# Second layer in quarters, most of its float64 weights converted beside it; twelve whole additions a pair feed summing products over three operands

## The chip, the core and the metric

The kernel runs on one core of a Trainium2 chip. TensorE (PE) multiplies matrices from on-chip memory (SBUF) into accumulators (PSUM); VectorE (DVE), ScalarE (ACT) and GpSimd (POOL) work on tiles element by element, POOL on SBUF alone; SyncE's queue (SP) issues the transfers (DMA). Each engine takes its instructions strictly in the order in which they were issued, so an instruction that waits holds up all that stand behind it on its engine. The metric is the device time of one execution in microseconds (us), as the median of the runs.

## The reference, cut to what matters

```python
q_pool = q.reshape(B, H, S // 2, 2, D).mean(axis=3)           # B 4, H 8, S 1152, D 64
attn = softmax(q_pool @ k.T / sqrt(D))                        # per head 576 x 1152
x = (attn @ v)                                                # 2304 tokens x 512
logits = x @ phi                                              # 32 slots, 4 for each of 8 experts
slot_input = softmax(logits, over tokens).T @ x
slot_out[e] = relu(slot_input[e] @ w1[e]) @ w2[e]             # w1, w2: 32 MB together
x = softmax(logits, over slots) @ slot_out                    # 2304 x 512
h = x @ w_in                                                  # w_in 512 x 2048, float64
g = where(h >= 1, h, where(h <= -1, 0, (h + 1) ** 2 / 4))
out = g @ w_out                                               # w_out 2048 x 512, float64
```

## The kernel before, in words

The program has three stages, and its instructions are issued by hand in the order in which they are to run.

**Attention.** Two heads make a pair `P`; there are 16 pairs, each of 9 steps `c` (128 keys) with two slots `h`. `at(g, slot, ...)` puts an action into a slot of step `g = 9 P + c`; "(c, h)" is a slot of a pair in what follows. A slot issues, in this order: the score products `mx` of a pair 11 steps ahead (`max_half`, line 305) and DVE's row maximum over them (line 317); this pair's scores `st` (line 371) and ACT's exponential `e` of them (line 376); at some slots the summing products (`es_sum`, line 394); the products with the values, `acc` (line 401); and then whatever was put into the slot. `mx`, `st` and some transposes share three PSUM buffers (`sc_p`), so the `st` of a slot takes the buffer that the `mx` of the slot ahead of it had, and must wait until DVE has read that `mx`.

The denominators are sums of `e` over the keys. `es_add` (line 384) adds the `e` tiles of several steps on DVE into `es`; `es_sum` multiplies the resulting operands with a column of ones on PE. `ADD` says in which slot which step's `e` is added, whole (0 to 2) or by halves; `GRP` groups the steps: 0 to 4 are added into one operand, 5, 6, 7 and 8 are operands of their own. `TAT` puts three operands behind the `st` of slot (7, 0) and two behind that of slot (0, 0) of the next pair. `PREP` places the preparation of later pairs (`prep_klo`, `prep_qp`, `prep_qlo`: four DVE instructions a pair).

**Conversion.** `w_in` and `w_out` come as float64. Each of 32 chunks of 128 x 512 is loaded (`cv_load`), and turned into float32 by one ACT instruction (`cv_abs`, line 191) and four on DVE (`cv_step`, lines 198 to 206: two with one operand and a constant, two with two operands). `CVS` puts all 32 into slots of the attention. The result goes back to DRAM (`wo_dr`, `wi_dr`) and is read again at the start of the last stage.

**Experts.** `w_load` fetches the 32 tiles of `w1` and `w2`, 1 MB each, into slots that `NWA` to `NW4` count, 23 of them; `w_last` goes into a tile that comes free later. The remaining 8 tiles, and behind them `wi_dr`, each wait until an earlier tile has been used (`w_used`). `h1` and `s2o` (lines 775, 827) are the products with `w1` and `w2`.

**Out stage.** `M = slot_out @ w_in` (line 924) is computed for all 2048 columns, so that `h = c @ M`; it is split in a high and a low part and repeated over partition groups (`Mrep`). Each of 9 blocks of 256 tokens has four units of 512 columns: products `h` (lines 968, 1014), an activation from ACT and DVE instructions (`h_unit`, `g_unit`), a split of the result into `ghi` (ACT) and `glo` (POOL, line 987, from two tiles in SBUF), and 24 products `po` (lines 1031 to 1033) with the split `w_out` (`whi`, `wlo`), which accumulate in PSUM over the four units of a block. `w_split` (lines 905, 907) makes `whi` and `wlo` on ACT, POOL and DVE at the start of the stage. `unit_step` runs the activations some units ahead of the products.

## Time and profile before

| | us |
|---|---|
| median of 3 runs (lowest, highest) | 782.45 (780.24, 783.18) |
| profiled execution, span from first to last instruction | 785.9 |
| attention, to the last summing products | 0 to about 502 |
| experts, to the last `s2o` | about 502 to 546 |
| start of the out stage | 546 to 573.6 |
| out stage, products without a break | 573.6 to 783 |

The profiled execution has no device time of its own beside its span, which lies 3.45 us above the median of the runs. PE is busy in 96% of the span, DVE in 74%, ACT in 57%, POOL in 16%. Busy times count an instruction from its start to its end; neighbours on one engine overlap by a little, so that the distance from one start to the next is less than the duration. In the view of stretches each engine has its busy time and, in brackets, its instructions, then follow the clock granted to TensorE (1.00 is 2.4 GHz, 0.50 is 1.2 GHz), the busy share of the DMA engines, and GB/s. In the view in order of time a row has start, duration, engine, line, operation, result and operands, shape and count, and in brackets the idle time ahead of it and what ended it; several instructions in a row can stand as one.

### The profile page before, as it was taken

To read this page: it belongs to the slowest core of one execution; us is meant where nothing else is said; L and a number is where in the kernel's file an instruction comes from. 1 tells how busy PE (TensorE), PEld (TensorE's weight loads), DVE (VectorE), ACT (ScalarE), POOL (GpSimd) and SP (SyncE) were. 2 spreads that over 40 slices of the span, in tenths; PEclk is the share of its full clock that TensorE was granted. 3 is DMA by queue.
4 is the path that set the end of the run, shared out by engine and by line. 5 is a ranking of instruction groups with operands and counts; after the bars stand their busy time and mean duration, and the time that the engine had idled before them with its cause. 6 is when DMAs were issued, how large, how long until landed. Compare 5 with 4: busy or idle time off the path is not lost.

```text
span 785.9 us, 19049 instructions
## 1 busy us (share of the span) xinstructions
PE 757.1 (96%) x7896; PEld 556.6 (71%) x7896; DVE 581.4 (74%) x947; ACT 451.7 (57%) x855; POOL 125.9 (16%) x100
## 2 busy tenths in 40 slices
...
GB/s 215 201 174 137 182 193 205 206 248 200 186 233 203 183 260 164 188 263 180 212 263 134 222 96 237 269 333 395 241 0 28 28 28 20 7 28 28 27 28 28
DMA packets 138263, 127.11 MB, mean 162 GB/s; under 512 B 80576, under 2 KB 100288, under 8 KB 137408
## 3 DMA queue, kind: packets, MB, share of 16 engines
...
HBM read 87.10 MB, written 13.11 MB: 128 GB/s over the span
## 4 chain that ended last, share of the span: by engine, by line
PE 60%; DMA 2%; DVE 2%; ACT 2%; issue 1%; SPq 0%; ACTq 0%; DVEq 0%
PE acc L401 9%; PE st L371 9%; PE po L1031 8%; PE po L1032 8%; PE po L1033 8%; PE mx L305 4%; PE acc L394 3%; DMA wi<-wi_dr 2%; PE h L968 2%; PE h L775 2%; PE tx L439 1%; PE tb L466 1%; DVE r L1021 1%; PE tr L428 1%; PE lp L482 0%
## 5 line engine op out<-in xcount | busy, mean ns | idle before, releaser
L376 ACT ACTIVATE e<-st 128x576 f32<-128x576 f32 x288 | 187.0, 651 | 139.0 <-PE st L371 125.6
L317 DVE TENSOR_REDUCE mp<-mx 128x1 f32<-128x576 f32 x282 | 212.1, 754 | 44.9 <-PE mx L305 38.0
L401 PE MATMUL acc<-e,vf 128*64 128x288 f32 x1152 | 195.1, 411 | 0.5 <-ACT e L376 0.5
L305 PE MATMUL mx<-K,q 128*64 128x288 f16 x1152 | 124.8, 298 | 9.6 <-DVE mp L317 3.4
L371 PE MATMUL st<-q,K 128*64 128x288 f16 x1152 | 122.0, 288 | 5.9 <-ACT e L376 4.7
L371 PE MATMUL st<-q,S 128*64 128x288 f16 x1152 | 122.0, 287 | 0.0
L305 PEld LDWEIGHTS <-q 128*64 128x64 f16 x1152 | 66.3, 112 | 70.2 <-issue 24.5
L1031 PE MATMUL po<-whi,ghi 128*128 128x512 f32 (+1 forms) x280 | 108.5, 388 | 0.0
L1032 PE MATMUL po<-wlo,ghi 128*128 128x512 f32 (+1 forms) x280 | 108.5, 388 | 0.0
L1033 PE MATMUL po<-whi,glo 128*128 128x512 f32 (+1 forms) x280 | 108.0, 386 | 0.0
L981 DVE TENSOR_TENSOR r<-cl,r 128x1024 f32<-128x1024 f32 x34 | 80.6, 2372 | 36.9 <-ACT cl L980 36.9
L987 POOL TENSOR_TENSOR glo<-r,ghi 128x1024 fp32r<-128x1024 f32 x34 | 82.2, 2417 | 95.3 <-ACT ghi L986 95.3
L401 PEld LDWEIGHTS acc<-e,vf 128*64 128x64 f32 x1152 | 77.4, 137 | 8.3 <-ACT e L376 2.0
L371 PEld LDWEIGHTS <-K 128*64 128x64 f16 x1152 | 68.3, 110 | 20.9 <-issue 12.7
L752 POOL MEMSET xfer<- 128x1024 f32 x1 | 1.0, 957 | 493.5 <-PE pb L562 493.5
L384 DVE TENSOR_TENSOR es<-es,e 128x288 f32<-128x288 f32 (+1 forms) x144 | 77.5, 550 | 2.2 <-ACT e L376 2.2
L371 PEld LDWEIGHTS <-S 128*64 128x64 f16 x1152 | 69.3, 110 | 3.4
L971 ACT ACTIVATE r<-h,cols 128x512 f32<-128x512 f32 x68 | 43.0, 685 | 31.4 <-PE h L968 31.4
L1033 PEld LDWEIGHTS po<-whi,glo 128*128 128x128 f32 x280 | 53.2, 190 | 10.8
L1031 PEld LDWEIGHTS po<-whi,ghi 128*128 128x128 f32 x280 | 53.4, 191 | 9.8
L1032 PEld LDWEIGHTS po<-wlo,ghi 128*128 128x128 f32 x280 | 53.3, 190 | 9.3
L972 DVE TENSOR_SCALAR cl<-h 128x512 f32<-128x512 f32 x68 | 43.8, 685 | 15.8 <-ACT r L971 13.9
(191 smaller groups left out, 854.1 us busy)
## 6 DMA issues: line engine op xcount, KB each, us to landing
...
```

The lines of the kernel that those rows point to most:

```text
L305: nc.tensor.matmul(ps[p0:p1, i, 0:HQ], lhsT=q1[P][:, t, p0:p1], rhs=kk[:, j * HQ:(j + 1) * HQ], start=True, stop=True)
L317: nc.vector.tensor_reduce(out=mp[P][:, t, a:a + 1], in_=ps[:, :, 0:HQ], op=ALU.max, axis=AX.XY)
L371: nc.tensor.matmul(ps[c0:c0 + 64, i, 0:HQ], lhsT=kk[:, ci, c0:c0 + 64], rhs=f[:, sl[i]], start=first, stop=not first)
L376: nc.scalar.activation(out=e, in_=ps[:, :, 0:HQ], func=AF.Exp, scale=ESC)
L384: nc.vector.tensor_tensor(out=Es[P, n, h][:, i0:i1], in0=a[:, i0:i1], in1=b[:, i0:i1], op=ALU.add)
L401: nc.tensor.matmul(acc[P, i][h * 64:(h + 1) * 64, 0:HQ], lhsT=vt[P][:, h, c, :], rhs=E[P, c, h][:, i, :], start=(c == 0), stop=(c == NK - ...
L972: nc.vector.tensor_scalar(out=cl[:, a:b], in0=src, scalar1=-1.0, scalar2=1.0, op0=ALU.max, op1=ALU.min)
L981: nc.vector.tensor_tensor(out=r[:, sl], in0=cl[:, sl], in1=r[:, sl], op=ALU.add)
L987: nc.gpsimd.tensor_tensor(out=glo[n, qd][:, sl], in0=r[:, sl], in1=ghi[n, qd][:, sl].bitcast(F32), op=ALU.subtract)
L1031: nc.tensor.matmul(po, lhsT=ghi[n, qd][:, j, sl], rhs=whi[:, f, cs], start=(f == 0), stop=False)
L1032: nc.tensor.matmul(po, lhsT=ghi[n, qd][:, j, sl], rhs=wlo[:, f, cs], start=False, stop=False)
L1033: nc.tensor.matmul(po, lhsT=glo[n, qd][:, j, sl], rhs=whi[:, f, cs], start=False, stop=(f == 15))
```

## The change

**Attention.** Steps 0 to 6 are added into one operand: twelve whole additions a pair, one in each slot from (2, 0) to (7, 1), where eight whole ones' worth were done in twelve instructions. The summing products have three operands, all behind the `st` of slot (0, 0) of the next pair. Of the conversions 12 of 32 chunks stay in the attention: two instructions a pair in the first slots, and one in each slot from step 6 of pair 14. The preparation moves by a few slots. **Experts.** Three tiles fewer are loaded ahead (20 instead of 23), and 11 instead of 8 wait for an earlier tile; `wi_dr` and `wo_dr` are gone, the converted weights stay in SBUF (`Wst`). **Out stage.** It runs over quarters `q` of the 2048 columns, and in a quarter over the 9 blocks: 36 units `k`. `M` is made a quarter at a time (`m_mm`, `m_rep`), each unit's 24 products end in PSUM and are added on DVE to partial results in SBUF (`o_out`). The other 20 chunks are converted in the units that `CVB` names, and split by `w_hi` (ACT) and `w_lo` (DVE). The activation is h clipped below at -1 plus (1 - clip(h)) squared over 4: two DVE instructions with an operand from PSUM take the place of one of 1024 columns from SBUF, and in odd units ACT clips.

```diff
-NWA, NW0, NW1, NW2, NWK, NW3, NW4 = 10, 2, 1, 6, 1, 2, 1
+NWA, NW0, NW1, NW2, NWK, NW3, NW4 = 10, 2, 1, 3, 1, 2, 1
...
+AHEAD = 3
+CVB = 1, 2, 3, 4, 5, 6, 7, 8, 9, 10, 11, 13, 14, 15, 17, 18, 19, 21, 22, 24
+MB = {1: 2, 2: 10, 3: 20}
...
-CVS = (0, 0), (0, 1), (1, 0), (1, 1), (3, 1), (7, 0), (7, 1), (8, 0), (8, 1)
+CVS = (0, 0), (0, 1)
+CVL = 4, 6
...
-GRP = ((0, 1, 2, 3, 4), (5,), (6,), (7,), (8,))
-TAT = ((7, 0, (1, 2, 0)), (9, 0, (3, 4)))
-ADD = ((4, 1, 0, 0, 2), (5, 1, 1, 0, 1), (6, 1, 1, 1, 2), (6, 2, 0, 0, 2), (7, 2, 1, 0, 2), (8, 3, 0, 0, 1), (9, 3, 0, 1, 2),
-       (10, 3, 1, 0, 2), (10, 4, 0, 0, 1), (11, 4, 0, 1, 2), (12, 4, 1, 0, 1), (13, 4, 1, 1, 2))
-PREP = (-20, -18, (-34, -33), -36, -16, -30), (-24, -22, (-41, -37), -41, -19, -37)
+GRP = ((0, 1, 2, 3, 4, 5, 6), (7,), (8,))
+TAT = (9, 0, (0, 1, 2)),
+ADD = tuple((2 * c + h + 2, c, h, 0, 2) for c in range(1, 7) for h in range(2))
+PREP = (-20, -18, (-34, -33), -36, -16, -30), (-24, -22, (-38, -36), -37, -18, -34)
...
-    wlist += [("wi", dc, 0) for dc in range(4)]
-    wo_dr = dr_p.tile([128, 16, DM], F32, name="wo_dr")
-    wi_dr = dr_p.tile([4, 128, DFF], F32, name="wi_dr")
...
+        qd, x = divmod(n, 8)
+        if x < 4:
+            src = w_in[x * 128:(x + 1) * 128, qd * 1024:(qd + 1) * 1024]
+            r0 = (4 * qd + x - 4) * 128
+            src = w_out[r0:r0 + 128, :]
+        nc.sync.dma_start(out=f64b[n % 2], in_=src.rearrange("p (f t) -> p f t", t=2))
+        cv[n] = f64b[n % 2], Wst[:, x - 4 if x >= 4 else 4 + 4 * (qd % 2) + x, :]
...
-            if n < 16:
-                nc.sync.dma_start(out=wo_dr[:, n, :], in_=dst)
-            else:
-                dc, qr = divmod(n - 16, 4)
-                nc.sync.dma_start(out=wi_dr[dc][:, qr * 512:(qr + 1) * 512], in_=dst)
-            if n + 3 < 32:
-                cv_load(n + 3)
+            if n + 2 < 32:
+                cv_load(n + 2)
...
-        cvs = [(NK * P + c, sl) for P in range(NP - 1) for c, sl in
-               CVS][CV0:]
-        for n in range(32):
+        for j in range(4):
+            at(NK * NP - 8 + j, 1, sel_build, j)
+        g1_ = NK * (NP - 1) - 3
+        cvs = [(NK * P + c, sl) for P in range(1, NP) for c, sl in CVS if NK * P + c < g1_]
+        cvs += [(g, sl) for g in range(g1_, NK * NP - 1) for sl in range(2)]
+        for n in range(12):
...
-        pieces = [(0, 2), (2, 4), (4, 8), (8, 12), (12, 16)]
-        for f0, f1 in pieces:
-            nc.sync.dma_start(out=wlo[:, f0:f1, :].bitcast(F32), in_=wo_dr[:, f0:f1, :])
...
+            if e < 4:
+                w_hi(0, e)
+            if 0 < e <= 4:
+                w_lo(0, e - 1)
...
+        def m_mm(q):
+            ps = po_tile(f"M{q}")[:, 0:128]
+            for dc in range(4):
+                for j in range(4):
+                    nc.tensor.matmul(ps[32 * j:32 * j + 32], lhsT=soT[:, dc, :],
+                                     rhs=Wst[:, 4 + 4 * (q % 2) + dc, j * 128:(j + 1) * 128], start=(dc == 0), stop=(dc == 3))
+            nc.scalar.activation(out=Mhl[:, 0], in_=ps, func=AF.Copy)
+            nc.vector.tensor_tensor(out=Mhl[:, 1], in0=ps, in1=Mhl[:, 0].bitcast(F32), op=ALU.subtract)
+        def m_rep(q):
+            Mst[q] = m_p.tile([128, 4, 128], F32R, tag="Mst", name=f"Mst{q}")
+            for a in range(2):
+                ps = po_tile(f"Mr{q}_{a}").rearrange("p (j x n) -> p j x n", j=2, x=2)
+                for j in range(2):
+                    nc.tensor.matmul(ps[:, j], lhsT=Sel[:, 2 * a + j, :], rhs=Mhl, start=True, stop=True)
+                for x, p0 in ((0, 0), (1, 64)):
+                    dst, src = Mst[q][p0:p0 + 64, 2 * a:2 * a + 2], ps[p0:p0 + 64, :, x]
+                    if x:
+                        nc.vector.tensor_copy(dst, src)
+                    else:
+                        nc.scalar.activation(out=dst, in_=src, func=AF.Copy)
...
+        def h_unit(k):
+            cl = t_p.tile([128, 4, TB], F32, tag="cl", name=f"cl{k}")
+            ps = []
+            for a in (0, 2):
+                ps.append(h_mm(k, a, a + 2))
+                if k % 2:
+                    nc.scalar.activation(out=cl[:, a:a + 2], in_=ps[-1], func=AF.Relu, scale=-1.0, bias=ones)
+                else:
+                    nc.vector.tensor_scalar(out=cl[:, a:a + 2], in0=ps[-1], scalar1=-1.0, scalar2=1.0, op0=ALU.max, op1=ALU.min)
...
+        def g_unit(k):
+            cl, ps = hq[k]
+            if k % 2:
+                nc.scalar.activation(out=cl, in_=cl, func=AF.Relu, scale=-1.0, bias=two)
+                nc.scalar.activation(out=cl, in_=cl, func=AF.Square, scale=-0.5, bias=ones)
+            else:
+                nc.scalar.activation(out=cl, in_=cl, func=AF.Square, scale=-0.5, bias=half)
+            r = hq[k] = t_p.tile([128, 4, TB], F32, tag="r", name=f"r{k}")
+            for a in (0, 2):
+                nc.vector.scalar_tensor_tensor(out=r[:, a:a + 2], in0=ps[a // 2], scalar=-1.0, in1=cl[:, a:a + 2], op0=ALU.max, op1=ALU.add)
...
+        def o_out(k, tt, po, c0=0, w=DM):
+            q, n = SEQ[k]
+            t = PA[2 * n + tt][:, c0:c0 + w]
+            if q:
+                nc.vector.tensor_tensor(out=t, in0=po, in1=t, op=ALU.add)
+            elif tt:
+                nc.vector.tensor_copy(t, po)
+            else:
+                nc.scalar.activation(out=t, in_=po, func=AF.Copy)
+            if q == 3:
+                r0 = n * TB + tt * 128
+                nc.sync.dma_start(out=out[r0:r0 + 128, c0:c0 + w], in_=t)
...
+            sp = split_of(k - 1)
+            ahead(k + AHEAD + 1)
+            if sp:
+                w_hi(*sp)
+            conv(k, 0, 2)
+            if k < len(SEQ) - 1:
+                o_part(k, 0, pos[0])
+                for q, b in MB.items():
+                    if k == b:
+                        m_mm(q)
+                    if k == b + 1:
+                        m_rep(q)
+                o_out(k, 0, pos[0])
+                conv(k, 2, 4)
+                if sp:
+                    w_lo(*sp)
+                o_part(k, 1, pos[1])
+                o_out(k, 1, pos[1])
+                conv_abs(k + 1)
```

On DVE, slots (6, 1) to (8, 1) of pair 7, before; `mx` and `mp` are the row maxima, `es` the additions, `mm` and `qn` close the maxima of a pair, `kn` and `qf` are preparation, `wst` conversion.

```order
L317 TENSOR_REDUCE mp_3656<-mx_8_1_4118 128x1
L350 TENSOR_TENSOR mm_4124<-mp_3656 128x9
L352 TENSOR_SCALAR qn_0_103<-mm_4124 128x9
L384 TENSOR_TENSOR es_0_1_3932<-es_0_1_3932,e_4_1_4041 128x288
L260 SCALAR_TENSOR_TENSOR kn_4075<-kf_3963,kn_4075 128x9x64
L273 TENSOR_TENSOR qf_3966<-qf_3966 128x9x64
L317 TENSOR_REDUCE mp_4145<-mx_0_0_4146 128x1
L206 SCALAR_TENSOR_TENSOR wst_3834<-f_15_3366,wst_3834 128x512
L317 TENSOR_REDUCE mp_4145<-mx_0_1_4195 128x1
L198 TENSOR_SCALAR wst_4193<-wst_4193 128x512
L317 TENSOR_REDUCE mp_4145<-mx_1_0_4215 128x1
```

And in the changed kernel, the same slots.

```order
L304 TENSOR_REDUCE mp_3450<-mx_8_1_3882 128x1
L337 TENSOR_TENSOR mm_3888<-mp_3450 128x9
L339 TENSOR_SCALAR qn_0_103<-mm_3888 128x9
L371 TENSOR_TENSOR es_0_1_3699<-es_0_1_3699,e_5_1_3856 128x576
L304 TENSOR_REDUCE mp_3907<-mx_0_0_3908 128x1
L371 TENSOR_TENSOR es_0_0_3673<-es_0_0_3673,e_6_0_3877 128x576
L304 TENSOR_REDUCE mp_3907<-mx_0_1_3928 128x1
L371 TENSOR_TENSOR es_0_1_3699<-es_0_1_3699,e_6_1_3902 128x576
L304 TENSOR_REDUCE mp_3907<-mx_1_0_3948 128x1
L247 SCALAR_TENSOR_TENSOR kn_3839<-kf_3729,kn_3839 128x9x64
L304 TENSOR_REDUCE mp_3907<-mx_1_1_3968 128x1
L260 TENSOR_TENSOR qf_3732<-qf_3732 128x9x64
```

Ahead of the maximum of slot (7, 0), the first with `mx_0_0`, stand `mm`, `qn` and a whole addition, where `mm`, `qn`, half an addition and two preparations stood. Each of the next two slots has a whole addition (the tail of the longer `es`) where a conversion instruction stood, and the preparations now stand one to a slot in step 8.

On SP's queue, the last loads of the experts and those of the out stage, before.

```order
L133 DMA w_3_1_8244<-in_moe_w_dram 128x4x512
L133 DMA w_4_1_8262<-in_moe_w_dram 128x4x512
L133 DMA w_5_1_8270<-in_moe_w_dram 128x4x512
L133 DMA w_6_1_8279<-in_moe_w_dram 128x4x512
L133 DMA w_7_1_8286<-in_moe_w_dram 128x4x512
L133 DMA wi_0_8292<-wi_dr 128x2048
L133 DMA wi_0_8298<-wi_dr 128x2048
L133 DMA wi_0_8313<-wi_dr 128x2048
L138 DMA wi_0_8325<-wi_dr 128x4x256 x2
L900 DMA wlo<-wo_dr 128x1024 x2
L900 DMA wlo<-wo_dr 128x2048 x3
```

And in the changed kernel, from `w_last` to the last tile of `w2`.

```order
L131 DMA w_last<-in_moe_w_dram 128x4x512
L131 DMA w_5_0_7767<-in_moe_w_dram 128x4x512
L131 DMA w_6_0_7773<-in_moe_w_dram 128x4x512
L131 DMA w_7_0_7779<-in_moe_w_dram 128x4x512
L131 DMA w_0_1_7785<-in_moe_w_dram 128x4x512
L131 DMA w_1_1_7803<-in_moe_w_dram 128x4x512
L131 DMA w_2_1_7811<-in_moe_w_dram 128x4x512
L131 DMA w_3_1_7820<-in_moe_w_dram 128x4x512
L131 DMA w_4_1_7827<-in_moe_w_dram 128x4x512
L131 DMA w_5_1_7833<-in_moe_w_dram 128x4x512
L131 DMA w_6_1_7839<-in_moe_w_dram 128x4x512
L131 DMA w_7_1_7854<-in_moe_w_dram 128x4x512
```

Eleven tiles of `w2` stand behind `w_last`, where eight tiles and four megabytes of `wi` stood (before, `w_5_0` to `w_7_0` stand ahead of `w_last`). Nothing of `wi` and `wlo` is left.

On DVE in the out stage, two units before (`cl` and `r` belong to the activation).

```order
L972 TENSOR_SCALAR cl_0_9236<-h_0_0_9237 128x512
L972 TENSOR_SCALAR cl_0_9236<-h_0_1_9242 128x512
L981 TENSOR_TENSOR r_3_9193<-cl_3_9194,r_3_9193 128x1024
L972 TENSOR_SCALAR cl_1_9286<-h_1_0_9287 128x512
L972 TENSOR_SCALAR cl_1_9286<-h_1_1_9292 128x512
L981 TENSOR_TENSOR r_0_9235<-cl_0_9236,r_0_9235 128x1024
```

And in the changed kernel, unit 10, which converts a chunk and splits another (`Wst` conversion, `wlo` split, `pa` the additions to the partial results).

```order
L967 SCALAR_TENSOR_TENSOR r_8981<-h_0_8916,cl_8915 128x512
L967 SCALAR_TENSOR_TENSOR r_8981<-h_2_8920,cl_8915 128x512
L190 TENSOR_SCALAR Wst<-Wst 128x512
L192 TENSOR_SCALAR Wst<-Wst 128x512
L1029 TENSOR_TENSOR pa_8053<-po_0_8965,pa_8053 128x512
L195 SCALAR_TENSOR_TENSOR Wst<-f_0_74,Wst 128x512
L198 SCALAR_TENSOR_TENSOR Wst<-f_0_74,Wst 128x512
L890 TENSOR_TENSOR wlo_7947<-Wst,whi_7946 128x512
L1029 TENSOR_TENSOR pa_8054<-po_1_8966,pa_8054 128x512
```

A unit had two instructions from PSUM and one addition of two SBUF tiles. Now it has two that read PSUM and SBUF, five that read SBUF alone, and two additions that wait for the unit's products.

## Rows read from the trace of the kernel before

**Rows 1.** Stretches: attention pair, experts, start of out stage, rest (core 0).

```profile
331.40:359.10 27.70, 27.70 (x386) 20.28 (x383) 26.24 (x48) 19.09 (x41) 0.00 (x0) 1.00 1.03 230
516.00:546.00 30.00, 29.85 (x275) 9.05 (x276) 12.55 (x47) 2.04 (x3) 5.24 (x33) 1.00 1.03 383
560.00:580.00 20.00, 15.95 (x61) 12.20 (x60) 17.04 (x25) 16.49 (x30) 15.74 (x12) 0.83 0.08 35
573.60:783.00 209.40, 209.00 (x1014) 176.63 (x1012) 127.92 (x103) 121.69 (x158) 88.92 (x38) 0.99 0.06 23
```

**Rows 2.** In order of time, PE, slots (0, 0) to (1, 0) and (7, 0) of a pair.

```profile
330.98 0.41 PE L305 MATMUL mx<-K,q 128*64 128x288 f16 x4
331.81 1.19 PE L394 MATMUL acc<-e,cols 128*32 128x192 f32 x32
333.46 0.41 PE L305 MATMUL mx<-K,q 128*64 128x288 f16 x4
334.68 0.41 PE L305 MATMUL mx<-K,q 128*64 128x288 f16 x4
...
352.10 0.41 PE L305 MATMUL mx<-K,q 128*64 128x288 f16 x4
355.07 0.41 PE L305 MATMUL mx<-K,q 128*64 128x288 f16 x4
```

**Rows 3.** In order of time, DVE, the same pair.

```profile
333.92 0.76 DVE L317 TENSOR_REDUCE mp<-mx 128x1 f32<-128x576 f32 x1 [0.18 <-PE mx L305]
334.59 0.68 DVE L203 SCALAR_TENSOR_TENSOR wst<-f,wst 128x512 int32<-128x512 int32 x1
...
352.12 0.17 DVE L350 TENSOR_TENSOR mm<-mp 128x9 f32<-128x9 f32 x1
352.33 0.19 DVE L352 TENSOR_SCALAR qn<-mm 128x9 f16<-128x9 f32 x1
352.41 0.45 DVE L384 TENSOR_TENSOR es<-es,e 128x288 f32<-128x288 f32 x1
352.78 0.75 DVE L260 SCALAR_TENSOR_TENSOR kn<-kf,kn 128x576 f16<-128x576 f32 x1
353.44 0.75 DVE L273 TENSOR_TENSOR qf<-qf 128x576 f32<-128x576 f32 x1
```

**Rows 4.** Groups by line and shape, 100 to 450 us; busy us, mean ns.

```profile
L384 DVE TENSOR_TENSOR es<-es,e 128x576 f32<-128x576 f32 x36 | 27.0, 750 | 0.0
L200 DVE TENSOR_SCALAR wst<-wst 128x512 int32<-128x512 int32 x27 | 11.3, 418 | 0.0
```

**Rows 5.** In order of time, SP's queue, last loads of the experts.

```profile
517.13 12.90 SPq L133 DMA_DIRECT2D w<-in_moe_w_dram  x8
534.71 3.50 SPq L138 DMA_DIRECT2D wi<-wi_dr  x2
```

**Rows 6.** In order of time, from the last `s2o` into the out stage.

```profile
545.87 0.69 DVE L910 COPY Prun<-s2o 128x512 f32<-128x512 f32 x1 [1.54 <-PE s2o L827]
548.32 1.07 PE L924 MATMUL M<-wi,soT 128*32 128x256 f32 x16
553.60 0.64 PE L924 MATMUL M<-wi,soT 128*32 128x256 f32 x8 [0.84 <-DMA wi<-wi_dr]
555.64 0.50 PE L1014 MATMUL h<-cT,Mst 128*128 128x256 f32 x2
559.92 0.62 PE L1040 MATMUL po<-whi,ghi 128*128 128x512 f32 x2
573.65 0.63 PE L1031 MATMUL po<-whi,ghi 128*128 128x512 f32 x1
```

**Rows 7.** Instructions of one line in the out stage: count, ns min/median/max.

```profile
L981 DVE TENSOR_TENSOR r<-cl,r x34: 1209/2421/2493, 576.4 to 751.7; 128x1024 f32<-128x1024 f32 x34
L987 POOL TENSOR_TENSOR glo<-r,ghi x34: 2391/2404/2849, 578.8 to 755.4; 128x1024 fp32r<-128x1024 f32 x34
L972 DVE TENSOR_SCALAR cl<-h x68: 676/682/692, 571.7 to 745.1; 128x512 f32<-128x512 f32 x68
```

**Rows 8.** In order of time, DVE and POOL in one unit of the out stage.

```profile
644.75 2.41 POOL L987 TENSOR_TENSOR glo<-r,ghi 128x1024 fp32r<-128x1024 f32 x1 [3.19 <-ACT ghi L986]
645.82 2.43 DVE L981 TENSOR_TENSOR r<-cl,r 128x1024 f32<-128x1024 f32 x1 [1.35 <-ACT cl L980]
```

309 lines of the change are left out of this document (120 added, 189 removed).

## The prediction

> **What bounds the kernel now.** I read the view of stretches first, to know which stage has which limit, then the order of time inside a pair of the attention, around the last loads of the experts and at the start of the out stage, and last the durations of single lines. In a pair of the attention (27.7 us) PE is busy throughout and DVE for 26.2; in the experts PE and the DMA engines are both full, at 383 GB/s; at the start of the out stage PE stands for a fifth of the time and the granted clock falls to 0.83; after that PE is full for 209 us, with DVE busy for 128, ACT for 122 and POOL for 89 [rows 1]. So PE is the bound in attention and out stage, and what I need to know is whether DVE, which the change loads differently, stays behind it. In the attention a slot without extras lasts 1.22 us (333.46 to 334.68); slot (0, 0) with two operands of summing products lasts 2.48, and slot (7, 0) with three 2.97 [rows 2]: 1.26 and 1.75 us for the products. All five are PE's time, nothing waits in them.
>
> **The attention, part by part.** The change leaves one place with three operands: 1.75 instead of 3.01 us a pair, **1.26 us less on PE in each of 16 pairs, 20.2 us** if nothing else moves.
>
> On DVE a maximum has .76 us, and the next instruction starts .67 after it; two preparations start .66 apart for .75 each [rows 3]. So an instruction costs its duration less some .08: whole addition .67 (750 ns), half one .37 (452 ns), conversion .60 or .34 [rows 3, 4]. Per pair: additions before 4 x .67 + 8 x .37 = 5.6, now 12 x .67 = 8.0; conversions before some 9 slots, 2.25 x (2 x .60 + 2 x .34) = 4.2, now a quarter of that, .9. DVE gets .9 us less work in a pair, PE 1.26 less: as a sum, DVE still fits.
>
> By slots it does not. In each of the slots (2, 0) to (7, 1) DVE now has a maximum and a whole addition, 1.34 us, where PE needs 1.22 unless transposes lengthen the slot, and in step 8 a preparation keeps it at 1.33. With three PSUM buffers the `st` of a slot needs the maximum of the slot ahead to be finished. A maximum starts .46 after its `mx` at the earliest (333.46 and 333.92 [rows 2, 3]), ends .76 later, and the `st` of the next slot is due 1.22 + .24 after that `mx`, so DVE may be late by about .2. Slot (5, 1) follows transposes and starts on time. Then the lag is .12 in (6, 0) and .24 in (6, 1); `mm` and `qn` (.3 together [rows 3]) and an addition make it about .7 in (7, 0). Before, this was the place of the three summing operands, which gave DVE 1.75 us behind a worse pile (`mm`, `qn`, half an addition, two preparations, to 354.11); they have moved away. PE waits .5 us there, and .12 more in each of (7, 1), (8, 0), (8, 1); slot (0, 0), now with 1.75 us of products, lets DVE catch up. **Stall: about .85 us a pair**, so .4 of 1.26 is left.
>
> It doesn't hold for all pairs. The three that carry the logits of a batch have other PE work in step 6 and begin step 7 without lag: 1.0 left, my choice between .4 and 1.26. Pairs 14 and 15 have no maxima in these slots: 1.26 each. Pair 13 has no preparation left in step 8: .6. Pair 0 is limited by its start: .5. The other nine: .4 each, 3.6. Sum 3.6 + 3.0 + 2.5 + .6 + .5 = **10.2 us gained**; the bounds are 20.2 (DVE never late) and about 0 (below).
>
> Chunks 7 to 11 are converted in the last step of slots, from two buffers, while three tiles of 1 MB load ahead of one of them: ACT and DVE may wait for it. Bounds: nothing, to one tile at 383 GB/s [rows 1], 2.7 us; I take **1 lost**, since PE can run on for two slots of `e`. The writes of converted chunks and most of their loads leave the pairs; the DMA engines were full there, but so was PE [rows 1], so I count nothing for it.
>
> **The experts.** Before, twelve megabyte tiles, eight of `w2` and four of `wi`, were asked for from 517.13 [rows 5] and the last was there at 553.60, where PE waited for it [rows 6]: 3.04 us each. Now eleven of `w2` come, and the last `s2o` needs the last of them: 517.1 + 11 x 3.04 = 550.6, plus .9 for its products: 551.5 instead of 545.8. **5.7 us later** (at 383 GB/s for each megabyte 3.4 less; nothing in the rows makes it sooner). From there before took 2.45 us to `M`, and stood until 553.60, then 2.04 to the first `h` at 555.64 [rows 6]. Now the quarter's `w_in` is in SBUF: 2.45 + .4 (the first products of a quarter of `M`) + 2.04 + .4 (transposes between) = 5.3, first `h` at 556.8.
>
> **The out stage.** Before, first `h` to first `po` took 4.3 us, and the steady products began only at 573.65 [rows 6], 18 us after the first `h`, because the splits of `w_out` (ACT, POOL and DVE at 85%, 82% and 79% [rows 1]) stood among the first activations. The change removes them from there: quarter 0 is split during `s2o`, where DVE is busy 12.6 of 30 us and ACT 2.0 [rows 1]; without this cover they would cost again some 5 us. I take 2.35 us to the first `po` (product, clip, square, addition, copy, .4 to .5 each) and no break after it. Before, the rest, 840 products `po` and 128 `h`, took from 573.65 to 782.6, 209 us (573.6 + 209.0 busy [rows 1]), part of it at half clock: the first took .63 us [rows 6]. Now 864 and 138: 209 x 864/840 = 215, plus 1 for ten more `h`. `m_mm` and `m_rep` for three later quarters: 1.4 each, 4.3 (the whole of `M` and its repetition are the same columns as before, only later). End: 556.8 + 2.35 + 220 = 779.2 instead of 782.6: **3.4 us gained** from here and the experts together. PE stands longer in the experts now (.9 us of products in each 3), and before, the clock fell after such a stretch (0.83, [rows 1]); I count **1 lost** for a slower start, bounds 0 and 3.
>
> DVE in this stage: a unit of PE is 209 / 35 = 6.0 us. By .60 for an instruction of 512 columns (as 682 ns [rows 7] less .08): two with PSUM and `cl` 1.2, clip in every other unit .6, two additions 1.2 (one in the first quarter): 3.0; with a chunk 1.9 more, with a `wlo` .6: 4.9 to 6.1. It fits if nothing holds it. But the old addition of two SBUF tiles took 1209 ns at its shortest and 2421 in the median, while instructions from PSUM never left 676 to 692 [rows 7]. POOL runs from 644.75 to 647.16, and DVE's addition, begun at 645.82, ends 1.09 after POOL's end: it stood still until POOL was done [rows 8]. Each chunk brings four instructions that read SBUF alone, and `wlo` a fifth. POOL runs 2.4 of 6.0 us, so each of the two clusters meets it with 4 in 10 and then waits 1.2 on average: 1.0 a unit, 5.9 to 7.1 in units with a chunk, over 6.0 only in units 9 to 11 or where a `wlo` falls; three units' lead absorbs that. **1 lost**, bounds 0 and 15.
>
> The Trainium skill, page "SBUF — State Buffer", section "SBUF: two separate sides", says the pair of ports that DVE and GpSimd share is an exclusive lock held for the whole instruction, for DVE instructions in a two-port mode or with two SBUF inputs. The trace agrees (1209 against 2421 ns). By that rule alone, with each conversion unit held for POOL's whole 2.4 us, the sum would come out as in rival C.
>
> **Sum**, against the span of 785.9: -10.2 + 1 - 3.4 + 1 + 1 = -10.6, so 775.3, and the median of the runs, 3.45 lower: **772**.
>
> **Rivals.** *A, DVE is never late where it counts*: the whole 20.2 us, 762. For it: DVE has .9 us less work in a pair. Against: 1.34 in a slot of 1.22, eleven times running. *B, the attention gains nothing*: if neighbouring additions don't overlap (.75 + .67 in a slot), the lag grows .2 a slot and the stall comes to 1.3 us or more, all of 1.26: 782, no change. For it: DVE was busy 26.2 of 27.7 us already; against: the starts .67 and .66 apart. *C, DVE becomes the bound of the out stage*: from 6.0 us a unit on. With 2.4 of waiting in each of the 20 units with a chunk, 7.0 in the first eight and 8.1 in units 9 to 11, 8 + 6 us, and about 7 more later, less some 6 that the lead and the units without a chunk take up: 15 lost, 787, slower. For it: the wait in [rows 8]; against: POOL is idle 6 parts in 10, and DVE's waits for `po` let it pass.
>
> **How the numbers follow.** Chances: mine .52, A .17, B .17, C .14. Around 772 my own case reaches from 767 to 778. A and half of B are to lie inside the range, C outside: 762 to 783. Half a per cent, 3.9 us, is about what a measurement of this kernel tells from no change: faster is below 778.5, slower above 786.4. Faster: A, nearly all of mine, a little of B: .69. Slower: most of C, .12. Same: the rest, .19.
>
> **What would show it.** In a plain pair after: period 27.3 (26.5 for A, 27.7 for B), waits of PE's `st` on DVE's maximum in (7, 0) to (8, 1) of some .85. The last `s2o` some 6 us later against the start of the experts than before. First `h` 5.3 us after it, no break behind the first `po`. In units 1 to 24 PE waits for `ghi`, `glo` or a `po` buffer below 2 us in all; if it waits at every unit with a chunk, C is right. I am wrong if the last chunks hold up the pairs 14 and 15 by more than 3 us, or if the half clock lasts through the first quarter.

## The result, and the profile after

The changed kernel takes 787.93 us (median of 6 runs, 784.35 to 790.12) against 782.64 (780.16 to 784.17): ratio 1.0072, 95% interval 1.0048 to 1.0097. A second comparison gave 1.0047 (1.0029 to 1.0064). It is slower by 4 to 6 us; the forecast was 772, faster by 10. An execution's device time lies 1.8 us above its span (786.93 for 785.1), so the profiled execution of before, with a span of 785.9, was longer than any of these six runs of its kernel. I therefore read the stages from two executions of each kernel.

| us, from ... to ... | before | before again | changed | changed again | forecast |
|---|---|---|---|---|---|
| start, last summing products of the first pair | 65.9 | 65.0 | 61.2 | 60.5 | 65.4 |
| the other 15 pairs | 435.2 | 433.8 | 425.0 | 426.4 | 426.5 |
| first `h` of the experts | 14.8 | 14.8 | 15.3 | 15.3 | 14.8 |
| end of the last `s2o` | 29.8 | 29.8 | 37.2 | 37.2 | 35.5 |
| first `po` | 14.1 | 14.1 | 10.8 | 11.3 | 7.7 |
| last product of PE | 222.7 | 222.6 | 232.5 | 231.2 | 222 |

Summing products, `h` and `po` are taken at their start, the last `s2o` and the last product at their end. The forecast of 426.5 is 435.2 less 9.7 for these pairs and plus 1; 222 is 220 with 1 each for the clock and for DVE. So the pairs came out as forecast, and the loss is in the last three rows. The stretches from the experts on, which answer to [rows 1]; columns as there:

```profile
501.50:520.00 18.50, 18.33 (x172) 5.59 (x174) 10.60 (x24) 2.04 (x3) 0.31 (x1) 1.00 1.02 368
520.00:549.50 29.50, 25.28 (x197) 12.54 (x195) 7.80 (x36) 7.21 (x17) 0.00 (x0) 0.77 0.53 194
549.50:570.00 20.50, 17.47 (x73) 14.39 (x73) 12.23 (x22) 13.33 (x22) 7.84 (x7) 0.83 0.09 26
570.00:783.00 213.00, 207.43 (x1052) 170.71 (x1050) 162.08 (x253) 127.01 (x157) 81.40 (x33) 1.00 0.18 64
```

Before, the granted clock was 1.00 through the experts; now it is 0.77 in the stretch that ends them. At the start of the out stage it is 0.83 in both kernels. In the rest PE stands 5.6 us, where it stood 0.4 before, and DVE is busy 162 instead of 128 us.

**A plain pair.** In order of time on PE, the maxima's products of slots (7, 0) to (8, 1), which answer to [rows 2]:

```profile
110.74 0.44 PE L292 MATMUL mx<-K,q 128*64 128x288 f16 x4
112.48 0.44 PE L292 MATMUL mx<-K,q 128*64 128x288 f16 x4
113.81 0.44 PE L292 MATMUL mx<-K,q 128*64 128x288 f16 x4
115.14 0.44 PE L292 MATMUL mx<-K,q 128*64 128x288 f16 x4
```

Slot (7, 0), 2.97 us before, lasts 1.74, and the next two 1.33 each where PE needs 1.22: .52 and twice .11 too long, as the forecast had it (.5 and .12).

**The end of the experts**, in order of time: SP's queue, then PE.

```profile
502.65 22.34 SPq L131 DMA_DIRECT2D w<-in_moe_w_dram  x11
...
528.73 1.07 PE L821 MATMUL s2o<-w,xfer 128*32 128x512 f32 x8 [0.84 <-DMA w<-in_moe_w_dram]
531.44 1.94 PE L821 MATMUL s2o<-w,xfer 128*32 128x512 f32 x8 [1.65 <-DMA w<-in_moe_w_dram]
534.15 1.93 PE L821 MATMUL s2o<-w,xfer 128*32 128x512 f32 x8 [0.78 <-DMA w<-in_moe_w_dram]
536.80 1.93 PE L821 MATMUL s2o<-w,xfer 128*32 128x512 f32 x8 [0.72 <-DMA w<-in_moe_w_dram]
538.67 1.54 PE L808 MATMUL ct<-ident,CN 96*128 96x96 f32 x8
547.14 0.85 PE L944 MATMUL h<-cT,Mst 128*128 128x256 f32 x4 [0.25 <-DVE Mst L936]
549.50 0.73 PE L1023 MATMUL po<-whi,ghi 128*128 128x512 f32 x2
```

PE waits for each of the last four tiles. After the first two waits the same products take 1.93 instead of 1.07 us: PE is at 1.2 GHz, from 531.2 to 544.8 by the granted clock, and the chain to the first `h` takes 8.4 us (transposes 1.54; .88 at full clock).

**A unit of the out stage** (unit 15), in order of time: the `h` that opens it and the next, POOL, DVE.

```profile
651.43 0.64 PE L944 MATMUL h<-cT,Mst 128*128 128x256 f32 x4
658.66 1.07 PE L944 MATMUL h<-cT,Mst 128*128 128x256 f32 x4 [1.12 <-DVE r L967]
...
652.88 2.69 POOL L977 TENSOR_TENSOR glo<-r,ghi 128x1024 fp32r<-128x1024 f32 x1 [2.25 <-ACT ghi L976]
...
653.22 2.90 DVE L890 TENSOR_TENSOR wlo<-Wst,whi 128x512 fp32r<-128x512 f32 x1
656.04 0.68 DVE L1029 TENSOR_TENSOR pa<-po,pa 128x512 f32<-128x512 f32 x1
656.64 1.27 DVE L955 TENSOR_SCALAR cl<-h 128x512 f32<-128x512 f32 x2
657.84 1.27 DVE L967 SCALAR_TENSOR_TENSOR r<-h,cl 128x512 f32<-128x512 f32 x2
```

A unit without waits lasts 5.94 us, or 7.17 and 6.44 where `M` and its repetition for the next quarter stand in it; this one has no `M` and lasts 7.23. DVE's split `wlo` needs .68 where it is alone; here it begins .34 us behind POOL's subtraction and ends .55 behind POOL's end. Behind it on DVE stand `pa`, the clip and then `r`, from which PE's `h` gets its PSUM buffer back: `h` waits 1.12. DVE's groups in the out stage (busy us, mean ns of one):

```profile
L195 DVE SCALAR_TENSOR_TENSOR Wst<-f,Wst 128x512 int32<-128x512 int32 x20 | 20.3, 1014 | 0.2
L198 DVE SCALAR_TENSOR_TENSOR Wst<-f,Wst 128x512 int32<-128x512 int32 x20 | 15.9, 797 | 0.7
L890 DVE TENSOR_TENSOR wlo<-Wst,whi 128x512 fp32r<-128x512 f32 x12 | 14.8, 1237 | 0.0
```

The means hide few long delays: seven of these 52 instructions (three of L195, one of L198, three of L890) take 2.8 to 2.9 us, each begun .1 to .5 behind POOL's subtraction; the others take .68 to .69. PE's waits for `r` (L967) come to 6.4 us in five places; the longest, 3.03, is in unit 1 (us in total, times, longest):

```profile
PE h L944 <- DVE r L967: 6.4, 5, 3.0
```

### The profile page after: what moved, and what is told of

It is laid out like the page before. It is cut to its first block, busy times and chain, and to the rows that moved or that the text cites. A ratio compares the mean times of both kernels' runs of the same rounds, so it can differ in the third digit from the quotient of the medians.

```text
span 785.1 us, 18089 instructions
## 1 busy us (share of the span) xinstructions
PE 749.0 (95%) x7422; PEld 551.6 (70%) x7422; DVE 610.7 (78%) x1024; ACT 447.3 (57%) x835; POOL 109.2 (14%) x74
## 5 line engine op out<-in xcount | busy, mean ns | idle before, releaser
L371 DVE TENSOR_TENSOR es<-es,e 128x576 f32<-128x576 f32 x160 | 119.7, 749 | 0.0
L292 PEld LDWEIGHTS <-q 128*64 128x64 f16 x1152 | 69.9, 110 | 63.0 <-issue 22.2
L1017 PE MATMUL po<-whi,ghi 128*128 128x512 f32 x280 | 110.5, 395 | 0.5 <-DVE pa L1029 0.3
L1017 PE MATMUL po<-wlo,ghi 128*128 128x512 f32 x280 | 109.9, 392 | 0.0
L1017 PE MATMUL po<-whi,glo 128*128 128x512 f32 x280 | 109.3, 390 | 0.0
L388 PEld LDWEIGHTS acc<-e,vf 128*64 128x64 f32 x1152 | 81.4, 137 | 5.3 <-ACT e L363 1.4
L358 PEld LDWEIGHTS <-S 128*64 128x64 f16 x1152 | 72.0, 110 | 2.8
L967 DVE SCALAR_TENSOR_TENSOR r<-h,cl 128x512 f32<-128x512 f32 x68 | 43.7, 685 | 35.6 <-ACT cl L964 25.1
L1017 PEld LDWEIGHTS po<-whi,ghi 128*128 128x128 f32 x280 | 53.2, 190 | 11.7 <-DVE pa L1029 0.5
L1017 PEld LDWEIGHTS po<-whi,glo 128*128 128x128 f32 x280 | 53.2, 190 | 11.3
L1029 DVE TENSOR_TENSOR pa<-po,pa 128x512 f32<-128x512 f32 (+1 forms) x54 | 36.7, 680 | 17.5 <-PE po L1017 17.4
L953 ACT ACTIVATE cl<-h,cols 128x512 f32<-128x512 f32 x34 | 21.6, 687 | 43.1 <-PE h L944 43.1
```

The costliest lines, as they stand in the source:

```text
L292: nc.tensor.matmul(ps[p0:p1, i, 0:HQ], lhsT=q1[P][:, t, p0:p1], rhs=kk[:, j * HQ:(j + 1) * HQ], start=True, stop=True)
L358: nc.tensor.matmul(ps[c0:c0 + 64, i, 0:HQ], lhsT=kk[:, ci, c0:c0 + 64], rhs=f[:, sl[i]], start=first, stop=not first)
L371: nc.vector.tensor_tensor(out=Es[P, n, h][:, i0:i1], in0=a[:, i0:i1], in1=b[:, i0:i1], op=ALU.add)
L388: nc.tensor.matmul(acc[P, i][h * 64:(h + 1) * 64, 0:HQ], lhsT=vt[P][:, h, c, :], rhs=E[P, c, h][:, i, :], start=(c == 0), stop=(c == NK - ...
L953: nc.scalar.activation(out=cl[:, a:a + 2], in_=ps[-1], func=AF.Relu, scale=-1.0, bias=ones)
L967: nc.vector.scalar_tensor_tensor(out=r[:, a:a + 2], in0=ps[a // 2], scalar=-1.0, in1=cl[:, a:a + 2], op0=ALU.max, op1=ALU.add)
```

## The experiments

Ratios are to the kernel before, with their 95% intervals; the changed kernel's is 1.0072 or 1.0047, so .001 is .8 us and a saving has two values. All edits are to the changed kernel but in the first run. Theories: **lock** (POOL makes DVE's conversions stand, and `r` is late), **clock** (waits for tiles bring TensorE to 1.2 GHz), **tiles** (eleven instead of eight behind `w_last`); against them, that PE's own work or the attention is the loss.

**e1_before_again**, no edit.

> The kernel before, unchanged, as one more profiled execution. The forecast was summed against a profiled execution whose span of 785.9 us lies 3.45 above the median of the runs, while the one of the changed kernel (785.1) lies below its runs. Theory 1 (most of that difference is TensorE at half clock in the first 66 us, where the old profile had 0.77 and 0.91 granted): this execution has a span of 779 to 782, its first pair ends about 61 to 62 us instead of 65.9, and from there to the last pair's end it takes 435 us again. Rival (the difference is spread over all stages): pairs of other lengths, 27.5 instead of 27.7 us. Ratio 1.000.

784.20 us, ratio 1.0013 (0.9998 to 1.0027), span 783.4. Half clock from 13 to 16, 23 to 30, 54 to 57 and 569 to 576 us, 20 us in all instead of 27. Neither expectation holds well: the first pair ends at 65.0, only .9 earlier, and the other pairs take 433.8. The old profile was a long execution in several places.

**e13_changed_again**, no edit.

> The changed kernel unchanged, as one more profiled execution, beside which the savings of the experiments can be read. If the stages found so far are the kernel's and not that one execution's: 425 us for the 15 pairs behind the first, 37 from the first h of the experts to the end of the last s2o, 10.8 from there to the first po, 231 to 233 from there to the last product, PE's waits for r 6.4 us, L195, L198 and wlo at 1014, 797 and 1237 ns; ratio 1.005 to 1.010. Rival (the stretches at half clock, other in each execution, make the difference): the last two stages differ by 3 us or more, and the ratio lies outside.

786.54 us, ratio 1.0047 (1.0029 to 1.0064), just below the 1.005 expected. The stages are those of the table, PE's waits for `r` again 6.4 us, `wlo` 1238 ns; L195 1119 and L198 692, so the delays change place a little between executions but come to the same. The losses are the kernel's. The half clock comes later here, at 536.5: of the last four `s2o` only the last takes 1.94 us, and yet it ends 37.2 us behind the first `h` again (the last two, in order of time). So the arrival of the tiles sets that end, and the clock adds its price to the last tile's products and to what follows.

```profile
534.79 1.07 PE L821 MATMUL s2o<-w,xfer 128*32 128x512 f32 x8 [1.65 <-DMA w<-in_moe_w_dram]
537.44 1.94 PE L821 MATMUL s2o<-w,xfer 128*32 128x512 f32 x8 [1.59 <-DMA w<-in_moe_w_dram]
```

**e3_no_convert**

```diff
-                for i in range(i0, i1):
-                    cv_step(cvb[k], i)
+                if i1 == 4 and cvb[k] + 2 < 32:
+                    cv_load(cvb[k] + 2)
```

> The changed kernel without the four DVE instructions of each of the 20 chunks in the out stage (it leaves out that conversion; their loads, the ACT step ahead of them and the splits stay). Theory DVE (conversions make r late, and h waits for its PSUM buffers): units of h take 5.9 to 6.0 us also between 617 and 729, the waits of h for r fall from 6.4 to about 1 us, in all 6 to 8 us less than the changed kernel, about 781. Rival (the out stage is longer by PE's own work, m_mm, m_rep and more products, and by the half clock): less than 2 us.

779.85 us, ratio 0.9961 (0.9945 to 0.9976): 6.7 to 8.7 us less. From the first `po` to the end 223.5 instead of 232.5; of PE's waits for `r` only the one in unit 1 is left (3.0). The conversions, planned to be hidden, cost that much; by what, the next run shows.

**e4_glo_const**

```diff
-            glo[k] = g_p.tile([128, 4, TB], F32R, tag="glo", name=f"glo{k}")
+            glo[k] = gl0
...
-            nc.gpsimd.tensor_tensor(out=glo[k], in0=r, in1=ghi[k].bitcast(F32), op=ALU.subtract)
```

> The changed kernel without POOL's subtractions in the out stage (glo is one constant tile of zeros; the products with it stay, so it leaves out the low part of g). Theory lock (DVE's conversions stand still while POOL runs): the last two conversion steps and wlo, 1014, 797 and 1237 ns in the mean, come back to 680, units take 6.0 us, and the whole is 5 to 7 us less than the changed kernel, nearly as without the conversions. Rival (DVE's own number of instructions is what makes r late): the waits of h for r stay at 4 us or more, and the time within 2 us of the changed kernel's.

779.59 us, ratio 0.9951 (0.9930 to 0.9973): 7.5 to 9.5 us less, with every conversion in place. The same groups as above:

```profile
L198 DVE SCALAR_TENSOR_TENSOR Wst<-f,Wst 128x512 int32<-128x512 int32 x20 | 13.8, 692 | 0.7
L195 DVE SCALAR_TENSOR_TENSOR Wst<-f,Wst 128x512 int32<-128x512 int32 x20 | 13.7, 686 | 0.2
L890 DVE TENSOR_TENSOR wlo<-Wst,whi 128x512 fp32r<-128x512 f32 x12 | 8.2, 684 | 0.0
```

All three are back at .69. In the changed kernel DVE stands 20 x .33 + 20 x .10 + 12 x .55 = 15 us in them; the out stage loses 7.6 of it (224.9 against 232.5). PE waits nowhere for POOL's `glo` in the changed kernel, so it is not POOL's own result that was late. DVE's own work doesn't limit the stage: the run without conversions is no faster than this one, and from the first wait in unit 1 on the units of both last the same, but for one that is longer here by 1.3 us of half clock.

**e6_late_split**

```diff
-            if 2 <= i - 2 < len(SEQ):
-                g_split(i - 2)
-            if 2 <= i - 1 < len(SEQ):
-                g_unit(i - 1)
+            steps = [(g_split, i - 2), (g_unit, i - 1)]
+            for f, x in steps[::-1] if i % 2 == 0 and i > 4 else steps:
+                if 2 <= x < len(SEQ):
+                    f(x)
```

> The changed kernel with one order on ACT turned round in the out stage: in every second unit ghi, and with it POOL's subtraction, comes behind the two steps of the next unit's square instead of ahead of them, some 2.3 us later. Nothing is left out. Theory lock (POOL runs while DVE does the last conversion steps and wlo, because ghi of every second unit comes ahead of PE): L195, L198 and L890 come down to below 800 ns in the mean, PE's waits for r fall to about 3 us, 6 to 9 us less than the changed kernel, 779 to 782. Rival (POOL meets the conversions wherever it is put, 4 parts in 10 of the time): the means stay at 1014, 797 and 1237 or trade places, and the time stays within 2 us.

783.30 us, ratio 0.9995 (0.9979 to 1.0011): 4.1 to 6.0 us less, the out stage 227.4. The groups:

```profile
L198 DVE SCALAR_TENSOR_TENSOR Wst<-f,Wst 128x512 int32<-128x512 int32 x20 | 15.9, 796 | 0.7
L190 DVE TENSOR_SCALAR Wst<-Wst 128x512 f32<-128x512 f32 x20 | 15.8, 789 | 0.0
L195 DVE SCALAR_TENSOR_TENSOR Wst<-f,Wst 128x512 int32<-128x512 int32 x20 | 13.7, 686 | 0.2
L890 DVE TENSOR_TENSOR wlo<-Wst,whi 128x512 fp32r<-128x512 f32 x12 | 10.4, 868 | 0.0
```

Half of each expectation: DVE still stands 11.7 us, but 7.4 of them now in L190 (419 ns without POOL), which is issued right behind `r`. PE's waits for `r` fall to 4.2, of which 3.0 are those of unit 1. So where the lock falls counts more than how long it is: ahead of `r` it reaches PE, behind `r` little of it does.

**e12_six_h_buffers**, and the same once more as **e14_six_h_again**.

```diff
-        po_p = ctx.enter_context(tc.tile_pool(name="po", bufs=4, space=PS))
+        po_p = ctx.enter_context(tc.tile_pool(name="po", bufs=2, space=PS))
+        hx_p = ctx.enter_context(tc.tile_pool(name="hx", bufs=2, space=PS))
...
-            ps = hp_tile(f"h{k}_{a}")
+            ps = (hx_tile if k % 3 == 2 else hp_tile)(f"h{k}_{a}")
```

> The changed kernel with six PSUM buffers for h and two for po (four and four before); M and its repetition use two of the h buffers and stand in units 3, 9 and 21 instead of 2, 10 and 20. Nothing is left out, and POOL and DVE stay in each other's way as before. The forecast said that three units' lead absorbs DVE's delays. Theory lead (with four buffers h of unit k+3 needs r of unit k+1, so that DVE may be late by less than one unit; with six it needs r of unit k): PE's waits for r fall from 6.4 us to below 1, also the one of 3.03 in unit 1, and the time is 6 to 9 us less than the changed kernel, 780 to 783, though L195, L198 and wlo stay near 1014, 797 and 1237 ns. Rival (DVE as a whole is behind, the lead doesn't matter): the waits move to po, which then waits for pa, and the time is within 2 us of the changed kernel's.

> The run with six buffers for h and two for po once more, for an undisturbed profile (the first one's span of 800.8 us is not that of its median). If DVE as a whole is behind and only the place of the wait changed: no wait of h for r, 10 us or more of waits of po for pa and of M for r, and a span of 788 to 792. If the loss came from elsewhere (the clock, the experts): the out stage from first po to last product is no longer than the changed kernel's 232.5 us.

793.20 and 795.39 us, ratios 1.0131 (1.0111 to 1.0151) and 1.0136 (1.0099 to 1.0173): slower. PE's waits in e14's out stage (us in total, times, longest):

```profile
PE po L1021 <- DVE pa L1033: 6.7, 10, 1.6
PE M L926 <- DVE r L971: 3.8, 2, 3.3
PE po L1021 <- ACT pa L1037: 2.2, 1, 2.2
PE po L1021 <- DVE pa L1035: 1.6, 1, 1.6
```

No `h` waits any more, but `po` does, and the stage takes 241.3 instead of 232.5; the span is 797.0, where 788 to 792 was expected, and one more stretch of half clock (583 to 586) has come in. My theory of the lead falls as far as it promised a gain: with fewer buffers for `po` the same lateness shows there. The rival has the place right and the time wrong (4.6 to 7.0 us more than the changed kernel, not within 2). Part of the loss is the edit's own, 3.8 us of waits of `M`, which it put onto the buffers of `h`; so these runs don't show how much lead alone is worth. Whether six buffers for `h` would help beside four for `po` wasn't tried.

**e2_warm** and **e7_warm_short**: products of the identity behind `s2o` of experts 3 to 6, first 6, 12, 12, 12, then 2, 5, 5, 5.

```diff
             s2o(e, 1)
+            warm_o(WS.get(e, 0))
```

> The changed kernel with 6, 12, 12 and 12 products of the identity behind the s2o of experts 3 to 6 of the second half, at the places where PE waits for a transfer. Theory clock (PE standing between the last products s2o brings the half clock of 530.7 to 544.4, and with it products of 1.9 us instead of 1.07 and a late first h): the half clock leaves this place, the last s2o ends about 1 us earlier, the first h follows it by 5 instead of 8.5 us, in all 4 to 5 us less than the changed kernel, about 783. Rival (the clock falls whatever PE does there, or falls later instead): no change, 787 to 788, or a half clock of the same length a few us later.

> The changed kernel with 2, 5, 5 and 5 products of the identity behind s2o of experts 3 to 6 (each takes .245 us, so 1.2 us where PE waited 1.65 at full clock; the earlier run had 2.9 us there, which put off each s2o by itself). Theory clock: no half clock in the experts, the last s2o 36 us behind the first h of the experts (37.2 in the changed kernel), first h of the out stage 6.2 us behind that (8.4), 3 to 4 us less, 784 to 785. Rival (half clock is only moved, to a later stretch of PE that is just as full): time within 1 us.

The first: 788.15 us, ratio 1.0071 (1.0056 to 1.0086), nothing gained. The granted clock did stay full there, and the first `po` came 8.1 us behind the last `s2o` instead of 10.8; but twelve products take 2.94 us and held up each `s2o` themselves (the last ends 40.5 instead of 37.2 us behind the first `h`). The second: 782.92 us, ratio 0.9992 (0.9978 to 1.0006), 4.3 to 6.3 less. PE, in order of time:

```profile
532.38 1.06 PE L822 MATMUL s2o<-w,xfer 128*32 128x512 f32 x8 [0.34 <-DMA w<-in_moe_w_dram]
533.37 1.38 PE L872 MATMUL s2o<-ident 128*128 128x128 f32 x10
...
537.74 1.07 PE L822 MATMUL s2o<-w,xfer 128*32 128x512 f32 x8 [0.27 <-DMA w<-in_moe_w_dram]
538.74 0.88 PE L809 MATMUL ct<-ident,CN 96*128 96x96 f32 x8
544.55 0.85 PE L946 MATMUL h<-cT,Mst 128*128 128x256 f32 x4 [0.26 <-DVE Mst L938]
```

The tiles come no sooner, but products take 1.07 and transposes .88 to the end, and the first `h` follows the last `s2o` by 5.7 us, near the forecast's 5.3. The half clock is not moved but shorter: 557 to 560 is all that is left of it at the start of the out stage.

**e10_eight_tiles**

```diff
+        if i >= len(wlist) - 3:
+            wt[kind, e, x] = wt[wlist[i - 3]]
+            return
```

> The changed kernel without the loads of the last three w2 tiles (it leaves them out: the last three s2o use the tiles of three experts earlier). It prices the term of the forecast that the last s2o comes 5.7 us later for eleven tiles behind w_last. Theory of the forecast with the half clock as found: PE no longer stands before the last s2o, the last s2o ends 29.8 to 30.5 us behind the first h of the experts as in the kernel before (37.2 in the changed kernel), no half clock there, the first h of the out stage 5.7 to 6.2 us behind it (8.4); in all 8 to 10 us less than the changed kernel, 779 to 781. Rival (PE is limited by something else, such as the order of SP's queue): less than 4 us.

776.90 us, ratio 0.9923 (0.9898 to 0.9948): 9.7 to 11.7 less, the largest single price. PE, in order of time:

```profile
529.18 3.64 PE L824 MATMUL s2o<-w,xfer 128*32 128x512 f32 x32 [0.62 <-DMA w<-in_moe_w_dram]
532.75 0.88 PE L811 MATMUL ct<-ident,CN 96*128 96x96 f32 x8
538.57 0.85 PE L947 MATMUL h<-cT,Mst 128*128 128x256 f32 x4 [0.26 <-DVE Mst L939]
```

The last `s2o` ends 30.6 us behind the first `h` of the experts (37.2), the first `po` 8.1 behind that (10.8), and the out stage takes 230.1 (232.5), since the half clock of 558 to 565 is gone too: 6.6 + 2.7 + 2.4 = 11.7.

**e9_no_later_m**

```diff
-                    if k == b:
-                        m_mm(q)
-                    if k == b + 1:
-                        m_rep(q)
+                    Mst[q] = Mst[0]
```

> The changed kernel without the products M, their split and their repetition for the three later quarters (it leaves out that part of the layer: all quarters use the first one's M). It prices the term that the forecast put at 4.3 us. Theory 1 (three times 1.73 us of PE's own work, as in the run with three things mended, where units 7.17 and 6.43 stand among units of 5.94): 5.2 us less than the changed kernel. Theory 2 (M also makes DVE late, whose Mhl and Mst stand among the conversions, so that part of the waits for r go with it): 7 us or more less. The forecast's term: 4.3.

785.85 us, ratio 1.0013 (0.9989 to 1.0037): 2.7 to 4.6 less. PE's waits for `r` rise to 8.1 us: while PE did `M`, DVE caught up. PE's own time for it is 5.2 (three times 1.73), of which 1.7 came back as waits; the time alone, with an interval of 2 us to either side, doesn't tell 5.2 from 4.3.

**e5_groups_back**: groups, slots and preparations of the kernel before.

```diff
-GRP = ((0, 1, 2, 3, 4, 5, 6), (7,), (8,))
-TAT = (9, 0, (0, 1, 2)),
+GRP = ((0, 1, 2, 3, 4), (5,), (6,), (7,), (8,))
+TAT = ((7, 0, (1, 2, 0)), (9, 0, (3, 4)))
```

> The changed kernel with the groups of additions, their slots, the summing products and the places of the preparations as before (five operands for the products, conversions and the rest as changed). Theory of the forecast (whole additions take 1.26 us of products off PE in a pair and give some .85 back as waits): plain pairs come back to 27.6 to 27.75 us from 27.45, the other pairs by 1 us, the end of the last pair 9 to 11 us later, 797 in all. Rival B (the attention gains nothing by the groups, and the conversions that left the pairs gave the gain): the end of the last pair within 3 us of the changed kernel's, 788 to 791.

792.09 us, ratio 1.0104 (1.0081 to 1.0128): 2.5 to 4.5 more. The 15 pairs take 431.7 us against 425.0, so the groups are worth 6.7, between the 9 to 11 of the forecast's theory and the rival's 3; in the out stage it is 3.0 faster (229.5 against 232.5), with waits for `r` of 5.3 and a shorter stretch of half clock. Slots (7, 0) and (7, 1) of a plain pair, on PE:

```profile
110.32 0.41 PE L293 MATMUL mx<-K,q 128*64 128x288 f16 x4
113.29 0.41 PE L293 MATMUL mx<-K,q 128*64 128x288 f16 x4
114.51 0.41 PE L293 MATMUL mx<-K,q 128*64 128x288 f16 x4
```

2.97 and 1.22 again; plain pairs last 27.75 instead of 27.45 us.

**e8_three_mended**: the edits of e6 and e7, and

```diff
-(nsteps - 9, g2x, NW2, "w2"),
+(nsteps - 5, g2x, NW2, "w2"),
```

> The changed kernel with three things mended: the turned order on ACT, the short products of the identity, and the three loads of the second last pool of weights asked for four steps of a pair later, behind the load of chunk 11 instead of ahead of it. If the three theories hold and add up: 6 to 9, 3 to 4 and 2 (the wait of PE's st behind ACT in the last pair) less than the changed kernel, 773 to 777, below the kernel before. Rival (the later loads put off the last s2o by what they save): 2 us more than that; if lock and clock are not the cause, 784 or more.

773.91 us, ratio 0.9878 (0.9857 to 0.9899): 13 to 15 less than the changed kernel, and 9.6 below the kernel before. The 15 pairs take 421.8 us (425.0), so the late chunk 11 had cost 3.2. The sum of the three single prices (4.1 to 6.0, 4.3 to 6.3 and 3.2) holds. The out stage takes 226.0, with units of 5.94 us but for those of the first wait and with `M`, and for four near 700 (7.23, 6.37, 6.16, 6.38), where a `wlo` and a conversion step still meet POOL and `h` waits 1.13. One in which PE is not held up, DVE then POOL:

```profile
605.99 1.28 DVE L969 SCALAR_TENSOR_TENSOR r<-h,cl 128x512 f32<-128x512 f32 x2
607.18 2.02 DVE L191 TENSOR_SCALAR Wst<-Wst 128x512 f32<-128x512 f32 x1
...
606.52 2.40 POOL L979 TENSOR_TENSOR glo<-r,ghi 128x1024 fp32r<-128x1024 f32 x1 [4.44 <-ACT ghi L978]
```

DVE stands here too, but `r` is done.

**e11_best_first**: e8, and in unit 1 the first twelve `po` ahead of the `h` of unit 4.

```diff
+            if k == 1:
+                o_part(k, 0, pos[0])
             ahead(k + AHEAD + 1)
```

> The run with three things mended, and in the out stage's second unit PE's first twelve products po ahead of the h of unit 4 instead of behind it. That h waits 3.03 us for DVE's r of unit 2, whose square stands on ACT behind the clip of unit 3. Theory (PE stands there for nothing, and the half clock of 551 to 556 follows from it): the wait falls below .7 us, 2.5 to 4 us less than the run with three things mended, 770 to 771.5. Rival (what h brings is needed as early, and the wait moves to the next units): within 1 us of 773.9.

775.12 us, ratio 0.9893 (0.9867 to 0.9919): nothing gained. That wait fell from 3.03 to .29 us and the half clock of 552 to 555 went, but the next `h` waits .90, a unit near 622 lasts 8.26, and the out stage takes 227.2 against 226.0. The rival held: the wait moved. In the long unit PE waits 1.64 us for DVE's `Mst`, which stands behind a conversion step that took 1.91 beside POOL: another order brought the two together in another place.

## Why the prediction was wrong

**The attention: right in its mechanism; its sum is in part luck.** The slots are too long by .52, .11 and .11 as worked out, and a plain pair lasts 27.45 (27.3 forecast). In the parts errors cancel. The groups are worth .3 in a plain pair (.4 forecast), .3 to .8 in the pairs with logits (1.0), and 6.2 in the 14 pairs between the first and the last (8.4). The conversions that left the pairs, which I counted at nothing, gave 4.6 to 6.1 in those 14 (403.9 in e5 against 408.5 and 410.0 before). The first pair gained 4 to 5 us that I had put at .5. A stretch of half clock from 53 on is gone from it; e9, which doesn't touch the attention, has it again (52 to 59), and its first pair ends at 63.2, where those of the other runs with these groups end at 59.8 to 61.9. By this one execution 1.4 to 3.4 of the 4 to 5 us go with that stretch; the rest stays open. Chunk 11 cost 3.2 instead of 1, over the bound of 2.7; in the other executions of the unmended loads the last pair takes 26.9 to 29.9 against 24.1 in e8, so 2.8 to 5.9. Of the forecast's signs of being wrong, the one on the last chunks (more than 3 us) thus came true. The load of 512 KB stood behind three tiles of 1 MB, as `wi` did in [rows 5], ACT waited for it, and PE behind ACT:

```profile
477.14 0.66 ACT L183 ACTIVATE Wst<-f 128x512 f32<-128x512 f32 x1 [3.57 <-DMA f<-in_moe_w_in_dram]
...
478.39 0.44 PE L358 MATMUL st<-q,K 128*64 128x288 f16 x4 [2.32 <-ACT e L363]
```

**The step that failed most: "three units' lead absorbs that".** The price of the lock was near in size (1.0 us a unit; measured 15 us in 20 units), but as an average it hid the form: seven delays of 2.1 to 2.2 us. That they would be hidden was wrong. With four PSUM buffers, `h` of unit k+3 needs `r` of unit k+1, so the lead on paper is three units and the one that DVE's lateness meets is less than one. And the meetings are not by chance, 4 in 10: ACT's order put POOL's subtraction of every second unit just where DVE has its last conversion steps and `wlo`, with the next `r` behind them. 7.6 us of the 15 reached PE, against 1 forecast; turning ACT's order took back 5.1 of the out stage with DVE standing 11.7 us still. It is rival C in half its size: not DVE's work (e3 is no faster than e4), but its place. That the median lies at C's 787 is a coincidence: the lock gave half of C's 15, other terms the rest. And the sign I had named for C, waits for `ghi`, `glo` or a `po` buffer, stayed at .3 us, below its 2: the wait came at the buffer of `h`, which the sign left out.

**Half clock: 1 forecast, 3 at most; measured 4 to 6.** I saw that PE would stand .9 of every 3 us at the end of the experts, and put the loss at the start of the out stage. It comes in the experts already: the last products, transposes and the first `M` run at half the clock (8.4 us instead of 5.7 to the first `h`), and another stretch follows from 558 to 565 (560 to 564 in the second execution). The Trainium skill, page "TensorE: Matmul & The Clock Gate", section "HAM oscillation — how this bites in real kernels", describes waits for a DMA between short groups of products, every one of which brings the clock back to half. The traces agree in part: 1.07 us, then 1.93 for the same products, but in the first execution only from the second wait on and in the second only after the fourth.

**The last `s2o`: mechanism right, size 7.4 for 5.7**; .9 of the difference is its own products at half clock. **First `h` to first `po`: 2.36 for 2.35. `M` of the later quarters: 5.2 for 4.3.** "No break behind the first `po`" was wrong: `h` of unit 4 stands 3.03 us behind `r` of unit 2. The kernel before has such a wait too, 2.96 us, but it ended at 572.46, just ahead of the 573.65 from which the forecast took its 209 us, so the sum left it out.

**How the miss adds up.** To PE's last product the changed execution takes 782.0 us where the forecast's stages add up to 771.9: 10.5 more in the out stage (the lock 6.6 beyond the 1 allowed, the wait in unit 1 3.0, `M` .9), 3.1 more to the first `po`, 1.7 at the last `s2o`, .5 ahead of the experts, less 4.2 in the first pair and 1.5 in the others. The other 6 of the 16 us between 772 and 787.93 lie in the last step of the sum, from span to median. I took off 3.45, the distance of the span of before from its median, and so set a span against device times; a device time is 1.8 longer than its span, and the changed kernel's profiled execution lay 1.0 below its median. Priced by experiments, the last three tiles with their clock cost 9.7 to 11.7 us (e10), the lock 7.5 to 9.5 (e4) and chunk 11 some 3, where the forecast had 5.7 + 1 + 1 + 1.
